# A fixed order for five engines: new words in the first layer, counted filler, and a new list for the expert layer

## The chip, the core and the metric

The kernel runs on one core of a Trainium2 chip. The core has a matrix engine (TensorE, PE in the profile), three engines for elementwise work (VectorE = DVE, ScalarE = ACT, GpSimd = POOL), a queue that only issues transfers here (SyncE = SP) and 16 DMA engines. The metric is the time of one execution on the device, in microseconds.

## What is computed

Three layers follow one another: pooled attention, a feed-forward layer with `h * cos(h)`, and a mixture of four experts, all in float32.

```python
# attention: 4 batches, 8 heads, 576 positions, head size 64, 32 memory slots
a = softmax(phi, axis=2)                       # over the positions
k_m = einsum('bhsm,bhsd->bhmd', a, k)
v_m = einsum('bhsm,bhsd->bhmd', a, v)
attn = softmax(matmul(q, k_m.T) / sqrt(64))    # over the 32 slots
x = matmul(attn, v_m)                          # then 2304 tokens x 512
# first feed-forward layer, 512 -> 2048 -> 512
h = x @ w_in
x = (h * cos(h)) @ w_out
# experts: 4 of 512 -> 1024 -> 512, weighted by domain_probs
p = domain_probs / domain_probs.sum(-1, keepdims=True)
for e in range(4):
    out += p[:, e:e+1] * (maximum(x @ w1[e], 0) @ w2[e])
```

## The kernel before

Nothing is scheduled by a compiler: the order of the instructions on every engine is written out in two tables of words. The work is cut into tasks, Python generators that yield one step (an `Op`) at a time. `Order.follow` reads the table word by word; each word names a task, and the task's next step is put on its engine. A step that two engines can do goes to the second one if the word has an apostrophe. Each engine runs its steps strictly in this order, and waits at a step until what the step needs is there. So a word's place sets what stands ahead of it on its engine, and nothing else.

`PLAN` (line 71) orders attention and the first feed-forward layer, with the first weights of the experts. Its tasks:

- `p`, `k`, `q`, `i`, `o` with digits are loads, one DMA each (a `k` is two, of 512 and 64 KB): phi, keys with values, queries, and slices of `w_in` and `w_out` as 64-bit words. p is 288 KB, q 576 KB, i and o 512 KB. All go through SP, which waits at a load until its buffer is free. There are 3 buffers for phi, 4 for k, 4 for q and 2 for raw weights (`RINGS`).
- `Abg` (`part`) is attention for batch b and group g of four heads: a maximum on DVE, the exponential on ACT, transposes on PE (`trans`, `pt`), pooling on PE (`pooled`, which needs both k of the group), a scaled copy on ACT (`kvs`), two transposes (`trans2`), a copy (`kvT`), scores on PE for either half of the positions (`score`, needs q), then a softmax over DVE, POOL and ACT (`sexp` is its exponential), a transpose, and a split in two parts for PE (`ahi` on ACT, `alo` on DVE or POOL).
- `wi`, `wo` (`narrow_in`, `narrow_out`) turn the 64-bit words into float32 weights on ACT and DVE.
- `P` (`project`) multiplies the pooled values by `w_in` (the values `vw`).
- `un.th` (`half`) is one unit of the first layer for half a batch: 12 matmuls (`hp`), then `h * cos(h)` in six steps, then four products `op` of six matmuls each with an addition (`ev`) each. `X` switches the on-chip memory over to the expert layer.

`LIST` (line 134) orders the expert layer: 64 units of a weight slice, two token groups each. `H` is the first product (with seven instead of eight block products), `R` the rectification, `P` and `Q` prepare the second product, `O` is the second product. For a pair of token tiles an `O` is PE's m1, m5, m6, m2, then a gather on DVE (e1: multiply by the expert's share and add to `acc`), then m7, m3, a second gather (e2), m4, and a third (e3). m7 overwrites what e1 reads, and m4 what e2 reads, so PE waits there for DVE. A single tile is one product `mm` and one gather. In the last two units, O62 (two pairs) and O63 (five tiles), each finished tile of the result is stored by a DMA of 256 KB on SP. `wa`, `wb`, `E`, `get`, `keep`, `fetch`, `park` and `unpark` build, store and load the weights' blocks and part of the accumulator.

PE also runs **filler**: matmuls of a 128x128 tile of ones whose result nobody reads, put ahead of steps at which PE waits. Each filler is two instructions in the trace. Fifteen run before the first word. In the kernel before, `Order.issue` reckons with its own cost figures how long PE will wait at a step that has a `fill`, and puts 0.75 of that time in filler ahead of it, plus counts from `more`; all of it before 75 us of its own reckoning.

Of the kernel before, what the change touches and what calls it, by code (L numbers as in the profile page):

```python
# [86 lines left out]
u2.0 u2.0 A30 A31 u2.1 A21 A31 u4.1 u2.1 u2.0 u3.1 u3.1 P4 u2.0 A31 A31 P4 u2.0 A30 A31 u2.1 u2.1 u4.1 u4.0 u2.1 A31
u3.1 u4.1 A30 u2.1 u2.1 u3.1 u2.0 A31 A30 u4.1 A30 u2.1 u2.0 wo2 u3.1 u3.1 u4.1 u3.1 A30 u3.1 u4.0 wi2 u3.1 u3.1
u4.1 u4.1' u4.0 X u4.0 G2 u6.1 wi2 wo2 u4.1 u6.1 u4.0 u6.1 u4.1' u4.0 u4.1 u6.1 wi2 u4.0' i21 u6.0 u4.0 G2 u6.1 G2'
G2' G2' u4.1' G2 u6.0 G2 u6.1 u6.0 u4.0' G2 u6.1' u4.0 wo2 G2 u6.0 G2 G2' u6.0 u4.0' G2 G2' u5.1 u6.0 u5.1 u6.1 G2  # L90
u6.1 wi2 u6.1 u6.0 u5.0 u6.0 u5.1 u5.1 u6.1' o21 wi2 u5.1 u5.0 wi2 u5.1 u5.0 G3 i30 u7.0 wo2 u5.1' u5.0 wo2 G2 u7.0
# [1801 lines left out]
```

## Time and profile before

| what | us |
|---|---|
| median of 3 runs | 1121.01 |
| lowest and highest | 1120.32, 1121.57 |
| the profiled execution | 1121.87 |
| its span, first to last instruction | 1120.1 |
| PE busy | 1104.5 |
| DVE, ACT, POOL busy | 865.1, 629.2, 577.7 |

The profiled execution is 0.86 us above the median; 1.8 us of it lie around the span. A matmul counts as busy from its start to its modelled end, and the next one starts before that end, so a busy PE is not PE at its peak: two starts must be compared. The trace holds every instruction in the order of the tables, so each one can be given to its word by counting.

### The profile page before, as it was taken

The page shows a single profiled execution, that of the slowest core. Times are in us where ns is not written, and L with a number is a line of the kernel's source. Part 1 is how long each engine was busy: PE and PEld are TensorE (multiplying, and loading weights), DVE is VectorE, ACT ScalarE, POOL GpSimd, SP SyncE. Part 2 cuts the span into 40 slices and gives each one's busy share as a digit, 9 for nine tenths or more (in the row PEclk, how much of TensorE's full clock was granted, in tenths as well). Part 3 has the DMA queues.
Part 4 walks back from the last instruction along what each step waited for, and adds up shares of the span by engine and source line. Part 5 has one row for each costly group of instructions (what it writes and reads, how often), then busy time and mean ns, then how long its engine had stood idle before and what let it go on. Part 6 is the DMA issues. An engine that isn't in the chain of part 4 may idle for free.

```text
span 1120.1 us, 22660 instructions
## 1 busy us (share of the span) xinstructions
PE 1104.5 (99%) x8981; PEld 1063.8 (95%) x8981; DVE 865.1 (77%) x1359; ACT 629.2 (56%) x1306; POOL 577.7 (52%) x569
## 2 busy tenths in 40 slices
...
GB/s 309 327 166 20 205 136 215 69 211 288 188 39 2 123 348 395 320 325 346 334 327 265 161 221 254 223 222 173 162 256 157 141 181 206 179 141 172 211 117 85
DMA packets 58554, 230.09 MB, mean 205 GB/s; under 512 B 6992, under 2 KB 17744, under 8 KB 44112
## 3 DMA queue, kind: packets, MB, share of 16 engines
...
## 4 chain that ended last, share of the span: by engine, by line
PE 90%; DVE 5%; DMA 2%; issue 1%; ACT 1%; POOL 0%; SPq 0%; DVEq 0%; ACTq 0%
PE op L506 48%; PE hp L506 33%; PE z L506 4%; DVE acc L1279 2%; PE vw_ps L793 1%; DVE ht L554 1%; PE spare L921 1%; DMA q<-in_qt_dram 1%; PE kvp L677 1%; DMA kv<-in_kv_dram 1%; PE sc L730 1%; DVE sm L554 1%; SPq L534 0%; DVE c L1265 0%; DVE acc L554 0%
## 5 line engine op out<-in xcount | busy, mean ns | idle before, releaser
L1279 DVE SCALAR_TENSOR_TENSOR acc<-op,p_all,acc 128x512 f32<-128x512 f32 x392 | 284.7, 746 | 120.9 <-PE op L506 118.7
L506 PE MATMUL hp<-x,wa 128*128 128x256 f32 (+1 forms) x2268 | 351.0, 295 | 0.1
L506 PEld LDWEIGHTS hp<-x,wa 128*128 128x128 f32 x2268 | 314.8, 188 | 2.0 <-DVE c L1265 0.3
L506 PE MATMUL op<-wt,ht 128*128 128x256 f32 x1464 | 228.8, 282 | 2.8 <-DVE acc L1279 2.6
L506 PE MATMUL op<-gt,wo 128*128 128x288 f32 x1536 | 218.1, 296 | 0.0
L506 PEld LDWEIGHTS op<-gt,wo 128*128 128x128 f32 x1536 | 208.1, 188 | 4.7 <-issue 2.4
L506 PEld LDWEIGHTS op<-wt,ht 128*128 128x128 f32 x1464 | 200.4, 188 | 5.6 <-DVE acc L1279 4.1
L506 PE MATMUL op<-wb,ht 128*128 128x256 f32 (+1 forms) x1182 | 203.2, 290 | 0.9 <-DVE acc L1279 0.8
L506 PEld LDWEIGHTS op<-wb,ht 128*128 128x128 f32 x1182 | 170.0, 188 | 5.9 <-DVE acc L1279 2.2
L554 POOL TENSOR_TENSOR sm<-c,sm 128x256 f32<-128x256 f32 x68 | 55.3, 814 | 145.8 <-DVE sm L554 118.8
L537 ACT ACTIVATE c<-c 128x256 f32<-128x256 f32 (+1 forms) x124 | 53.7, 443 | 126.7 <-DVE c L1265 126.6
L506 PE MATMUL hp<-attnT,vw 128*128 128x288 f32 x768 | 114.5, 298 | 0.3 <-DVE attnT L554 0.3
L554 POOL TENSOR_TENSOR ht<-sm,ht 128x512 fp32r<-128x512 f32 x72 | 97.8, 1366 | 31.8 <-ACT ht L537 28.2
L506 PEld LDWEIGHTS hp<-attnT,vw 128*128 128x128 f32 x768 | 106.4, 190 | 3.9 <-issue 2.0
L554 POOL TENSOR_TENSOR gt<-y,gt 128x576 fp32r<-128x576 f32 x41 | 60.0, 1463 | 79.2 <-ACT gt L537 76.2
L900 DVE TENSOR_TENSOR acc<-op,acc 128x576 f32<-128x576 f32 (+1 forms) x120 | 84.9, 711 | 17.3 <-PE op L506 16.1
L554 POOL TENSOR_TENSOR sm<-c 128x512 f32<-128x512 f32 x23 | 30.2, 1313 | 100.2 <-ACT c L537 83.5
L537 ACT ACTIVATE ht<-sm 128x512 fp32r<-128x512 f32 x122 | 75.2, 625 | 11.4 <-POOL sm L554 7.7
L554 POOL TENSOR_TENSOR ht<-c,ht 128x256 fp32r<-128x256 f32 (+1 forms) x61 | 67.1, 1105 | 25.1 <-ACT ht L537 25.1
L1265 DVE TENSOR_TENSOR c<-hp,u 128x320 f32<-128x320 f32 (+1 forms) x126 | 56.5, 453 | 22.0 <-PE hp L506 20.5
L537 ACT ACTIVATE ht<-c 128x256 fp32r<-128x256 f32 (+1 forms) x129 | 63.8, 516 | 13.6 <-PE op L506 12.2
L537 ACT ACTIVATE u<-hp 128x320 f32<-128x320 f32 (+1 forms) x126 | 50.5, 407 | 35.8 <-PE hp L506 35.5
...
## 6 DMA issues: line engine op xcount, KB each, us to landing
...
```

The lines of the kernel that those rows point to most:

```text
L506: nc.tensor.matmul(out=ps, lhsT=lt(a), rhs=rt(b), start=first and i == 0, stop=last and i == 2, skip_group_check=more,)
L537: return Op("ACT", ns, fn or (lambda: nc.scalar.activation(out=out, in_=in_, func=func, **kw)), *deps, table=table)
L554: eng.tensor_tensor(out=out, in0=in0, in1=in1, op=op)
L677: nc.tensor.matmul(out=kvp[32 * i:32 * i + 32], lhsT=es[:n, c, 32 * i:32 * i + 32], rhs=kv[i // 2][0][0][:, c, i % 2] if c < NC else kv[i ...
L730: nc.tensor.matmul(out=sc[32 * i:32 * i + 32, :TH], lhsT=kvT[b][p0:p0 + 64, 0, i, :], rhs=qt[p0:p0 + 64, i, :], start=True, stop=True,)
L793: nc.tensor.matmul(out=ps[32 * i:32 * i + 32, g, j * FS:j * FS + FS], lhsT=kvT[b][64 * g:64 * g + 64, 1, i, :], rhs=wi[s][0][64 * g:64 * g ...
L900: e = yield dve(155 + 301 * nd, lambda: nc.vector.tensor_tensor(out=dst, in0=op[:, :, :TH], in1=dst, op=ALU.add), o)
L921: nc.tensor.matmul(out=bank, lhsT=ones, rhs=ones, start=True, stop=True, skip_group_check=True)
L1265: return dve(157 + 1.045 * n, lambda: nc.vector.tensor_tensor(out=out, in0=ps, in1=sb, op=ALU.add), *deps)
L1279: nc.vector.scalar_tensor_tensor(out=dst, in0=ps, scalar=pe, in1=dst, op0=ALU.mult, op1=ALU.add)
```

## The change

Three things change, in the tables and in how filler is counted; no step is added or taken away, and each engine's total of steps stays but for those that move between two engines.

1. `PLAN` has the same 1462 words in another order (25 with the apostrophe set differently). Loads are among them: k000, k001 stand right behind p00; i00, i01 behind k011; q01, o00, i10 and p31 later, k110, k100 and k101 earlier. After the eighth unit the order on PE is that of before.
2. Filler is no longer reckoned. `FILLS` gives the count for each of PE's first 37 steps, 42 fillers in all (the trace of before holds 57).
3. `LIST` has the same 3646 words in another order, with 135 apostrophes set differently. Most words move by fewer than 10 places. At its end the products of O62 and O63 and the nine stores stand in another order.

```diff
--- before.py
+++ after.py
 PLAN = """
-p00 p11 k001 A00 k001 A00 A00 k000 A00' k000 A00 A00' A00 A00 A00 A00 p01 q00 A01 p10 i00 A11 A00' A10 A00 A00 q01
-A01 A01 A11 A00 A00' A00 A11 A01' A11 o00 A01 k010 A11 k010 A00 A01 k011 wi0 A10 k011 p20 A00 wi0 A00 A00 wi0 A00
-i01 A00 k111 A00 A00 p21 A01 A00 k110 k111 A01 A11' wo0 k110 wo0 A00 A11 A00 wo0 A00 A01 A00 A10 wi0 A01 A20 A00 o01
-A00 A00 wi0 A01 A01 A10 wi0 A01 A00 i10 P0 A01 A10 k100 A20 A01 P0 k100 A01 A21 P0 A01 A21 A01 k101 A11 A01' A01
-A10' A11 A01 A01 k101 p31 A10 A01 A20 A20 wo0 A11 q10 wi1 A20 A01 A20' A11 u0.0 A01 wo0 A01' wi1 A10 A01 A21 u0.0
-wo0 A01 u0.0 A01 wo0 wi1 u0.0 A11 q11 A01 A31 A01 A10 wo0 p30 A10 A11 A21 A01 u0.0 A10 k200 k200 A11 A11 k201 wo0
-A10 k201 wo0 A11 A01 i11 wo0 A10 u0.0 k210 A10 A30 A11 A21 A31 A10 A11 A30 P1 u0.0 wi1 A10 A10 A20 k211 A21 A11 u0.1
-A20 A11 A20 u0.0 wi1 A20 A10 u0.0' u0.1 u0.0 k210 u0.0' A20' A11 A21 A10 wi1 k211 u0.0 A21 q20 u0.0' P1 A10 A11 u0.1
-A11 A21 k301 P1 u0.0 u0.0' A31 A10 A11 A21 q21 A31' A20 A21 A30 k301 A10 o10 A20 u0.1 A31 A21 k300 P2 A10 A30 A20
-A21 A21 u0.1 A10' A20 A30 u0.1 P2 u0.1' u1.0 A21 u1.0 u0.1 wo1 u0.1' P2 u0.1 u1.1 u1.0 wo1 wo1 u1.0 u1.0 u0.1' u1.1
-A21 o11 u1.0 u1.1 u0.1 u0.1' u0.1 wo1 u1.1 u1.0 u3.0 A30' u1.0 A20 u0.1 u1.1 u1.0 u3.0 q31 k311 u1.1 A20 u1.1 u1.0
-u3.0 u1.0' q30 A31 i20 u1.0 u1.0 wo1 u3.0 A20 u3.0 u1.0 P3 wo1 A21 u1.0' k300 k310 A30 A20 P3 A20 wo1 A20 u1.1 A31
...
+p00 k000 k001 k000 k001 p01 q00 p10 A00 k010 A00 A00 A00 A00 p11 A00 A00 k010 A00 k011 A01 k011 i00 A00 A01 i01 A00
+A00 A10 q01 A00 A01 A00 A01 A01 k111 A00 A00 A11 p20 k111 A01 A11 A01 A00 A10 A01 A00 A00 A00 wi0 wi0 A01 wi0 A01 A00
+A11 o00 A01' wi0 wi0 k110 k110 A11 A11 A01 wi0 k100 A00 A01 A11' o01 A00 A00 A11 P0 A01 A00 A01 A10 A00 A01 A10' A10
+p21 A00 P0 k101 A01 A00 k101 A10' A00 A00 k100 P0 A00 A01 A00 A01 q10 A20 A11 A00 q11 wo0 A00' A20 A01 p31 A10 wo0 A01
+A11 A01 A01 A20 A01 wo0 A11 A20 wo0 A20 u0.0 A01 p30 A11' A20 A01 wo0 i10 A01 A21 k200 u0.0 A10 k200 wo0 k201 A01 wo0
+A01 k201 A11 A01' A21 wo0 A01 u0.0 A10 wo0 A01 A10 A20 i11 wo0 A11 A11 A10 A21 k211 wo0 A11 P1 u0.0 A11 A01 k211 A10
+A21 u0.0 A11 P1 A10 A10 u0.0 u0.1 k210 A10 A10 u0.0 A31 k210 A21 A11 q20 A30 A10 u0.0 wi1 A11 u0.1 q21 A11 A10 wi1 A11
+u0.0' u0.0 A20 A21 A10 A31 wi1 A30 A10 o10 A20 A10 u0.0' u0.0 A20 wi1 wi1 A11 A30 u0.1 A20' A11 wi1 u0.0' u0.0 A11 P1
+o11 k300 A21 A21 A30' P2 k300 u0.1 A10 k301 A21 A20 k301 u0.1 u0.0' A21 k311 A10 A31 A20 q30 A20 A21' A10' u0.1 A21
+A20 P2 A30 u0.1 u1.0 k310 A21 P2 k310 u0.1 u1.0 A20 wo1 u1.1 u1.0 A20 k311 u0.1 q31 u1.0 u0.1 A31 u1.0 u1.1 A21 wo1
+u1.0 u1.1 u3.0 A30' u0.1' u1.0 A21 u1.1 A30 A21 u0.1 u3.0 u1.1 u1.0 u3.0 u1.1 wo1 P3 u0.1' u1.1 u3.0 i20 A31 A30 A31
+u3.0 A21 u1.0 A20 u1.0 A31 A20 A21 u2.0 u1.0 A30 wo1 wo1 A21 P3 u0.1 wo1 A20 A30 o20 u1.0 u0.1' P3 A20 u3.0 u1.1 A30'
...
 LIST = """
...
-P62' O61.2 P62 P62 H63 O61.1 O61.0 O61.0 H63 H63 O61.0 P62' O61.1 O61.0 O61.1 O61.0 H63 H63 O61.0 P62' O61.1 O61.1
-O61.0 H63 O61.0 O61.1 H63 H63 R63 O61.1 O62.0 O61.1 H63 R63 R63 O62.0 R63 O62.1 O62.0 O62.1 R63 O62.0 O62.1 O62.0
-Q63.0 O62.1 Q63.1 Q63.0' O62.1 Q63.2 Q63.1' Q63.3 O63.0 O62.0 Q63.4 Q63.3 Q63.4' Q63.2 O62.0 O63.0 O62.0 O63.1 O62.0
-O62.1 O63.2 O63.1 O63.3 O63.2 O62.1 O62.1 O63.4 O62.1 O63.3 O62.1 O62.1 O62.0 O63.4 O62.0 O63.3 O62.1 O63.0 O62.0
-O62.1 O63.2 O62.0 O63.1 O63.4
...
+O61.2 O61.1 O61.0 O61.0 O61.1 O61.0 H63 O61.1 O61.0 H63 H63 R63 O61.0 O61.1 R63 R63 H63 O61.1 R63 O62.0 R63 O62.0
+O62.1 O62.0 O62.1 Q63.0 O62.0 O62.1 Q63.0 O62.0 Q63.1 O62.1 Q63.2 Q63.1' O62.1 Q63.3 O62.0 Q63.4 O63.0 Q63.3 Q63.2'
+Q63.4 O62.1 O63.1 O63.0 O62.0 O62.1 O62.1 O63.2 O62.1 O63.1 O62.1 O62.0 O63.0 O63.2 O63.3 O62.0 O63.2 O62.0 O63.4
+O63.3 O63.1 O63.3 O62.0 O63.4 O62.1 O62.1 O63.4 O62.0 O62.1 O62.0
 """.split()
...
@@ -324,8 +322,10 @@
 DMA_NS = 1.0 / 362.0
 DMA_LAG = 2700.0
 DMA_OPEN = 8
-FILL, FILL_NS, FILL_END = 0.75, 215.0, 75000.0
-LATE, LATE_NS = (14000.0, 35000.0), 1000.0
+FILLS = (
+    0, 0, 3, 3, 2, 0, 0, 10, 4, 0, 1, 0, 1, 0, 0, 0, 10, 0, 0, 0, 0, 0, 1, 0, 3, 0, 0, 0, 0, 0, 0, 0, 2, 0, 0,
+    0, 2,
+)
 
 
 class Order:
@@ -341,7 +341,7 @@
         self.left = {}
         self.quiet = set()
         self.log = []
-        self.more = [0, 0, 2, 0, 4]
+        self.fills = list(FILLS)
         self.stall, self.slack, self.late = 0.0, ({},) * 4, False
 
     def add(self, name, rank, gen):
@@ -410,13 +410,11 @@
             op.end = self.bus + DMA_LAG * 0.5
             self.landed.append(op.end)
         else:
-            if op.fill and t < FILL_END:
+            if op.fill:
                 bank, free = (self.spare, None) if self.spare is not None else op.fill
-                late = max((d.end + LATE_NS for d in op.deps if "SP" in getattr(d, "engs", ("SP",)) and LATE[0] < d.end < LATE[1]), default=0.0)
                 if task[3][0] == "P":
-                    self.spare, late = None, 0.0
-                more = self.more.pop(0) if self.more else 0
-                for _ in range(more + int(FILL * (max(t, late) - max(self.at[eng], free.end if free else 0.0)) / FILL_NS)):
+                    self.spare = None
+                for _ in range(self.fills.pop(0) if self.fills else 0):
                     self.filler(bank)
             self.at[eng] = t + ns
             if eng in op.port:
```

The order of PE's, DVE's and SP's last steps, read from the end of either table:

```
PE before   O62.1:m2 O63.0 O62.0:m7 O62.0:m3 O63.1 O63.2 O63.3 O62.1:m7 O62.1:m3 O63.4 O62.1:m4 O62.0:m4
PE after    O62.1:m2 O63.0 O63.1 O62.0:m7 O62.1:m7 O62.1:m3 O63.2 O62.0:m3 O63.3 O63.4 O62.0:m4 O62.1:m4
DVE before  O62.0:e1 O63.0 O62.0:e2 O62.1:e1 O63.1 O63.2 O62.1:e2 O63.3 O63.4 O62.1:e3 O62.0:e3
DVE after   O62.0:e1 O62.1:e1 O63.0 O62.1:e2 O63.1 O63.2 O62.0:e2 O63.3 O63.4 O62.1:e3 O62.0:e3
SP before   O62.1:e2 O62.0:e2 O63.3 O63.0 O62.1:e3 O63.2 O62.0:e3 O63.1 O63.4
SP after    O62.1:e2 O63.0 O63.2 O62.0:e2 O63.1 O63.3 O63.4 O62.1:e3 O62.0:e3
```

(SP's words are the stores; each is named by the gather that it waits for.)

## Rows read from the trace of the kernel before

**Rows 1.** Page, part 1: busy us, share of the span, instructions.
```profile
PE 1104.5 (99%) x8981; PEld 1063.8 (95%) x8981; DVE 865.1 (77%) x1359; ACT 629.2 (56%) x1306; POOL 577.7 (52%) x569
```

**Rows 2.** Stretches: us, busy of PE, PEld, DVE, ACT, POOL; clock, DMA share, GB/s.
```profile
0.00:10.00 10.00, 7.87 (x73) 7.71 (x76) 1.83 (x5) 2.61 (x5) 0.70 (x6) 1.00 0.80 268
10.00:20.00 10.00, 10.00 (x107) 8.29 (x97) 7.60 (x19) 5.78 (x14) 1.61 (x3) 1.00 0.97 340
20.00:30.00 10.00, 10.00 (x163) 7.92 (x162) 8.11 (x21) 5.61 (x13) 3.12 (x4) 1.00 0.99 337
30.00:40.00 10.00, 7.96 (x94) 5.36 (x96) 8.76 (x22) 9.22 (x15) 5.23 (x7) 0.96 1.04 361
40.00:50.00 10.00, 10.00 (x104) 7.12 (x97) 5.89 (x16) 5.42 (x13) 4.84 (x4) 0.70 0.95 309
50.00:60.00 10.00, 9.75 (x146) 7.20 (x145) 9.07 (x18) 8.14 (x14) 2.57 (x2) 1.00 0.93 329
60.00:130.00 70.00, 69.95 (x687) 64.87 (x692) 61.91 (x111) 52.67 (x86) 39.24 (x37) 1.00 0.34 109
```

**Rows 3.** Groups of PE instructions on ones (L921): busy us, mean ns, idle before.
```profile
L921 PE MATMUL spare<-ones 128*128 128x128 f32 x92 | 12.3, 278 | 0.0
...
L921 PE MATMUL kvp<-ones 128*128 128x128 f32 x16 | 2.1, 275 | 0.0
L921 PE MATMUL sc<-ones 128*128 128x128 f32 x6 | 1.2, 324 | 0.0
```

**Rows 4.** Timeline of PE, 5 to 60 us: start, us, instruction, count [idle before].
```profile
27.77 1.08 PE L677 MATMUL kvp<-kv,es 128*32 128x128 f32 x32
...
31.35 0.30 PE L658 MATMUL pt<-ident,phi 128*64 128x128 f32 x1 [1.04 <-ACT es L551]
31.41 1.82 PE L506 MATMUL hp<-attnT,vw 128*128 128x288 f32 x12
33.07 0.83 PE L921 MATMUL kvp<-ones 128*128 128x128 f32 x6
...
38.35 0.69 PE L730 MATMUL sc<-q,kvT 64*32 64x288 f32 x8 [0.64 <-DMA q<-in_qt_dram]
...
41.97 1.11 PE L793 MATMUL vw_ps<-wi,kvT 64*32 64x256 f32 x16
43.00 3.19 PE L506 MATMUL hp<-attnT,vw 128*128 128x288 f32 x12
46.13 1.08 PE L677 MATMUL kvp<-kv,es 128*32 128x128 f32 x32
...
50.28 1.08 PE L677 MATMUL kvp<-kv,es 128*32 128x128 f32 x32
...
51.65 1.06 PE L506 MATMUL op<-gt,wo 128*128 128x288 f32 x6
...
53.29 0.69 PE L730 MATMUL sc<-q,kvT 64*32 64x288 f32 x8
53.93 0.66 PE L651 MATMUL pe<-ident,phi 128*128 128x128 f32 x4
...
58.94 1.34 PE L506 MATMUL op<-gt,wo 128*128 128x288 f32 x9
```

**Rows 5.** Timeline of DVE, 43 to 51 us.
```profile
48.78 0.75 DVE L747 TENSOR_REDUCE ssm<-st 128x18 f32<-128x576 f32 x1 [3.52 <-ACT st L537]
```

**Rows 6.** PE's waits from 130 us on: us, times, longest.
```profile
PE op L506 <- DVE acc L1279: 3.5, 7, 0.9
```

**Rows 7.** Timeline of the end.
```profile
1110.75 3.47 DVE L1279 SCALAR_TENSOR_TENSOR acc<-op,p_all,acc 128x512 f32<-128x512 f32 x5 [1.36 <-PE op L506]
1111.53 5.16 SPq L534 DMA_DIRECT2D out_dram<-acc  x9
```

**Rows 8.** DMA issues near 1111.5 (first store) and 1116 us: count, KB, us to landing.
```profile
out_dram<-acc SPq DMA_DIRECT2D x1, 256.0 KB, 2.1
...
out_dram<-acc SPq DMA_DIRECT2D x2, 256.0 KB, 3.0
```

More of the change, by code (lines that the diff above doesn't have):

```diff
@@ L87 @@
[L87 to L91, printed above, removed]
@@ new lines @@
+u1.0 u1.1 u3.0 A30' u0.1' u1.0 A21 u1.1 A30 A21 u0.1 u3.0 u1.1 u1.0 u3.0 u1.1 wo1 P3 u0.1' u1.1 u3.0 i20 A31 A30 A31
+u3.0 A21 u1.0 A20 u1.0 A31 A20 A21 u2.0 u1.0 A30 wo1 wo1 A21 P3 u0.1 wo1 A20 A30 o20 u1.0 u0.1' P3 A20 u3.0 u1.1 A30'
+u2.0 A31 u1.0' u1.1 wo1 A20 u2.0 A30 A31 wo1 A30 A30 u2.1 A30 u3.0' u2.0 A30 u1.0 u2.1 A21 u2.0 A20 u1.1 A21 u2.1 A31
+u3.1 u1.1' wo1 u1.0 A31' u2.1 A20' wo1 u2.1 u3.1 wo1 A21 A31 u2.0 A31 A31 P4 A21 u2.0 A31 wo2 u1.1 A31 u3.0 u3.1 u1.1'
+A31 u3.1 u3.0 u3.0 A30 u3.0 u3.0 u1.1 A21 u3.0 A31 u3.1 u2.0 u1.1' A31 P4 u2.0 u2.0 A30 A31 u3.0 u2.0 u2.1 A31 P4 u2.0
@@ L133 @@
+u29.1 R1 u29.1 R1 u28.0 u28.1 u30.1 R1 u29.1 u30.1 u29.1 u30.1 u28.1 u28.1 R1 u30.1 u29.0 R1 u28.1 u29.1 B u29.0 B
+u30.1 u29.0 u31.1 u30.1' u29.0 B u29.1 u29.1 u31.1 u29.0 u31.1 B u29.0 u30.1 u29.1 u31.1 R1 u31.1 B u30.0 u29.0 u31.1
+u30.1 B' B u31.1 u30.1 u30.0 B' u31.0 R1 B' R1 u29.0 u30.0 B u30.1 u31.0 B u31.0 u29.0 u29.0 u31.0 u30.0 u31.0 u31.1
+u29.0 u31.0 B u31.0 u31.1 u31.1 u30.0 B u31.0 u30.0 u31.1 B u30.0 u31.0 u31.0 B' B u30.0 B u31.0 B u30.0 u30.0 u30.0
 """.split()
 LIST = """
[L135 removed]
@@ new lines @@
+wb11' R21 O20.1 wb11' wb11 O20.0 O20.0 P21' H22 P21 wb11' P21 O20.1 H22 O20.0 O20.1 wb11' P21 P21 H22 P21 O20.1 H22
+wa12' wb12 O20.0 P21 P21 O20.1 O20.0 H22 H22 H22 O20.0 O20.1 P21' P21 O20.1 O20.0 P21 H22 O20.1 H22 O20.0 wa12 O20.1
+H22 R22 O21.0 O20.1 O21.0 H22 R22 wa12' O21.1 keepwa11 wa12' wa12 wa12 R22 Q21.2 O21.0 R22 R22 O21.1 Q21.2' unpark
+wa12 O21.0 wa12' O21.0 O21.2 P22' P22 wa12' O21.1 wa12' H23 P22' O21.0 P22 P22 P22 H23 H23 P22' P22 P22 O21.1 O21.2
+O21.1 H23 H23 wa12' O21.0 O21.1 H23 H23 O21.0 O21.1 O21.0 O21.1 H23 O21.1 O21.0 O21.1 O21.0 H23 wb12 wa13 wb12 wb12
@@ new lines @@
+P22 P22 wb12 H23 H24 wb12' R23 R23 wb12 O22.0 O21.1 O22.0 H23 wb12' wb12 R23 wb12 O22.0 wb12' R23 O22.1 keepwb11 R23
+O22.1 O22.0 O22.1 O22.0 P23 H24 H24 P23 O22.0 O22.1 H24 H24 wa13 wb13 O22.1 H24 P23 O22.0 O22.0 P23 P23 P23 P23' H24
+O22.1 O22.1 O22.1 H24 P23 P23' O22.0 P23 O22.1 O22.0 P23 H24 H24 R24 Q23.2 O22.0 O22.1 R24 R24 H24 Q23.2 O22.1 R24
+O23.0 wa13 keepwa12 R24 O23.0 keepwt11 P24 P24 O23.1 wa13' O23.2 O23.0 P24' wa13 O23.0 P24' P24 P24 H25 O23.2 O23.0
+O23.1 P24' H25 H25 wa13 P24 P24' P24 O23.0 H25 H25 O23.1 wa13 H25 wa13 wa13' wa13 O23.0 P24 H25 O23.1 O23.0 O23.1
```

375 lines of the change are left out of this document (181 added, 194 removed).

## Prediction

> **What bounds the kernel now.** I read the page's busy shares first, then stretches of the span, then TensorE's timeline of the first 60 us, its waits, and the end. PE is busy for 1104.5 of 1120.1 us [rows 1], so time can come off only where PE runs filler, runs slowly, waits, or has stopped. There are three such places. *The start:* from 30 to 50 us PE lists 94 and 104 matmuls in 10 us, the granted clock is 0.96 and 0.70 of full, and the DMA engines are busy 0.97 to 1.04 of their time from 10 to 40 us [rows 2]. Matmuls on ones (filler) cost 12.3 + 2.1 + 1.2 = 15.6 us [rows 3]. So the start is bound by loads, and by half a clock after a thin stretch of PE. *The middle:* from 60 us on PE is busy all the time [rows 2], but waits seven times for a DVE gather, 3.5 us together [rows 6]. *The end:* the last gathers end at 1110.75 + 3.47 = 1114.22 us, yet nine stores are issued in one row from 1111.53 to 1116.69 [rows 7]; the last is issued one mean issue (5.16 / 9 = 0.57) before, near 1116.1, and lands 3.0 us later [rows 8], at 1119.1.
>
> The profiled execution took 1121.87 us (span 1120.1, 1.8 around it). The median is 1121.01, 0.86 lower. The sum below is made in the profiled execution and moved down by that 0.86.
>
> **Part 1: order of the first layer and counts of ones.** I go by landings. Sizes are from the code: p 288 KB, k 512 + 64, q 576, i and o 512. A load lands when the bytes up to its end have moved, by the GB/s of the stretches [rows 2], plus a lag. The lag has one good row: A11's second scores start at 38.35 us, after waiting for q11 [rows 4]. The list of before has 11,488 KB = 11.76 MB up to q11, moved at 36.4, so the lag is 1.9 us (an estimate, +-0.6). The stretches move 2.68, 3.40, 3.37, 3.61 and 3.09 MB, so 6.08 MB by 20 us, 9.45 by 30, 13.06 by 40.
>
> Landings in the new order: k110's tail (7,584 KB = 7.77 MB) 25.0 + 1.9 = 26.9. Last tail of k10 (9,536 KB) 32.8. q10 (10,112 KB) 34.4. q11 (10,688 KB, since i10 and p31 no longer stand ahead) 36.0. k201's tail (12,928 KB) 42.5. k210's tail (14,592 KB) 48.0. q21 (15,744 KB) 51.8. From k200 to i11 the bytes ahead are those of before, so these land no earlier: PE only stops being behind its loads.
>
> PE in the new order. Durations are from start to start [rows 4]: pooled 1.37 (50.28 to 51.65), hp 1.66 (31.41 to 33.07), so an op of six matmuls 0.83, scores 0.64 (53.29 to 53.93), four transposes 0.5 and two 0.25 (estimated from their row), a vw 1.0 (41.97 to 43.00); two ones 0.27 (12.3 / 46 [rows 3]). A11's pooled matmuls wait for k110 and run 26.9 to 28.3 (before from 27.77). Scores, transposes and u0.0's hp follow, near 30.0 to 31.6 (before from 31.41). A10 pooled waits for k10: 32.8 to 34.2; A11's scores wait for q10, 34.4, and q11, 36.0 to 36.6 (before from 38.35). A21's transposes 0.5, P1 1.0, two scores 1.3: u0.1's hp runs 39.4 to 41.1. Before, it ran from 43.00 for 3.19 us at half clock. A pt, ones and two ops (2.2) end at 43.3, A20 pooled at 44.7 (before 46.13 + 1.37 = 47.5). Op, ones, transposes and op (2.9) end at 47.6; now **PE waits for k210**: A21 pooled 48.0 to 49.4 (before to 51.65). P2 1.0, scores 0.64, transposes 0.75, then scores behind q21, 51.8 to 52.4, scores 0.64, a pt: u1.0's hp runs 53.2 to 54.9. Before, the first op after it starts at 58.94 [rows 4]. The new order has by then left A21's second scores and A31's pt (0.74) for later, so it stands where before stood at 58.94 when it is 55.6: **the lead is 3.3 us**. Bounds, from 0.6 of lag either way and an attention chain up to 1 us late: 1.8 to 5.0.
>
> What else that needs. DVE must bring A10's attention (its last step `alo`) by 53.2. Before, DVE stood 3.52 us until 48.78 for ACT's exponential of A10 [rows 5], which was queued on ACT behind a step that needs A20 pooled (46.13 [rows 4]). In the new ACT order it stands ahead of that step, so this stall goes. What is late next is A10's `ahi`, on ACT behind A21's `kvs`, which needs A21 pooled (49.4): kvs, an eviction and ahi (estimates of 0.5 to 0.7 each), then `alo` (0.7, as DVE's other steps of this shape [rows 5]), end near 52.1, 1.1 before it is needed.
>
> Moves on other queues. *SP:* p11 now stands ahead of k010's tail and waits for a phi buffer that A00's pt frees, within the first 10 us; 3,104 KB are queued ahead, moved only at 11.5, so the DMA engines don't run dry. o00 stands ahead of k110 and waits for i00's narrowing, near 19.5; 6,496 KB ahead are moved at 21.7. *ACT:* A01's `kvs` now stands behind the narrowing of i00 (4,544 KB, landing 17.7), and A01's transposes, its first scores and u0.0's hp behind that. PE waits for k110 until 26.9 anyway, which hides it; without that cover, the nearest row is PE's wait of 1.04 us for ACT at 31.35 [rows 4]. I take 0 and keep +1.0, which is in the bounds. *POOL* gets the same kinds of steps in another order: 0.
>
> The ones: 57 before (114 instructions in [rows 3], two each), 42 in the new list, so 15 x 0.27 = 4.0 us fewer. They stand where PE waits for a load, so alone they are worth nothing; ten remain ahead of A01's and of A11's pooled matmuls. What they do bear on is the clock. It lost 0.04 x 10 / 0.5 = 0.8 us from 30 to 40 and 6.0 us from 40 to 50 [rows 2], so it ran at 1.2 instead of 2.4 GHz from about 39.2 to 46.0, after PE had waited for ACT at 31.35 and for q11 at 38.35 with little between [rows 4]. The Trainium skill ("TensorE: Matmul & The Clock Gate", section "HAM oscillation — how this bites in real kernels") says that short bursts of matmuls between DMA waits throttle the array again and again; it speaks against fewer ones, and by it the sum would be rival A's.
>
> **Part 2: list of the expert layer.** *The end.* PE's last products are the same (O63.4, then an m4 of each pair of O62), so the last gather ends at 1114.22 + 0.1, as O62.1's now waits for the very last m4. What changes is who is queued behind whom on SP. Before, SP's first word is the store after O62.1's second gather, the seventh of the last eleven gathers, and eight stores stand behind it. In the new list O62.1's m7 and m3 come before O63.2, this gather is the fourth of eleven, and the stores nearly follow the gathers, the two last ones last. Gathers come every 3.47 / 5 = 0.69 us and an issue takes 0.57 [rows 7], so no store waits for another: the last is issued at 1114.35. Landing takes between 2.1 (the first, queues empty) and 3.0 us (the last two of nine) [rows 8]; I take 2.4, nearer the first, as few stores are under way: 1116.75 instead of 1119.1. **Gain 2.35**, bounds 1.7 and 2.7.
>
> *The rest of the list.* Most words move a few places, and 135 change between POOL and DVE. The seven waits [rows 6] come from gathers queued behind DVE steps; for three of them (O8.1, O23.1, O29.0) the new list puts 0.4 to 0.7 us more PE work between product and reader. Ends: all seven go (-3.5), or as many come (+3.5). I take 0, as kinds and numbers of steps are the same. The weights' transfers keep their order but for neighbours; `unpark`'s second half and two stores of unit 29 move far down, where they were due long before.
>
> **Sum.** 1121.87 - 3.3 - 2.35 + 0 = 1116.2 in a profiled execution; less 0.86: **1115.3**.
>
> **Rivals.** *A, the clock still falls* between 31 and 46 us. For: fewer ones, and PE still waits near 31.6, 34.2 and 35.5. Against: hp, scores and vw stand closer together than before. Price: u0.1's hp 3.19 instead of 1.66, 1.5 us, or P1, scores and pooled about as much; the waits for k210 take part of it: 1.2 to 1.8. Time 1116.8. *B, the lead is given back before 130 us:* DVE is busy 9.07 of 10 us from 50 on and 61.9 of 70 after that [rows 2], so it may become the bound, and only the end is left: 1121.0 - 2.35 = 1118.7. Against: DVE's 3.52 us stall goes. *C, slower:* the reordered list makes PE wait for gathers (m7, m4) more often. A wait is 0.5 us on average [rows 6]; to cancel 5.7 us and be 2.3 slower takes 16 more of them among the 122 pairs of products: 1123.3. Against: a doubling (seven more, 1118.8) is the most that the unchanged kinds of steps suggest. *D, more than forecast:* loads land 0.6 earlier, and half of the seven waits go: 1112.7.
>
> **How the numbers follow.** Forecast 0.57, with its own range 1113.6 to 1117.0; A 0.13; B or C's doubling 0.14; C 0.05; D 0.11. The range takes in A, D's near side and half of B: 1112.5 to 1118.4. Within 0.2% of 1121.0 (1118.8 to 1123.2, about what a measurement can tell from no change) lie half of B and the short side of C, 0.11; slower 0.04; faster 0.85.
>
> **What would show it.** Right: A21 pooled starts within 0.8 us of 48.0; u0.1's hp takes 1.7 us at full clock; u1.0's hp ends near 54.9; the nine stores go out one by one, and the last lands about 2.5 us after the last gather's end. Wrong: a PEclk below 0.9 before 50 us (A), PE waiting for DVE between 55 and 130 us (B), more than 7 us of waits for `acc` (C), a landing 3 us or more after the last issue.

## The result, and the profile after

The changed kernel takes 1109.0 us (1108.8 to 1109.6, four executions) against 1121.3 of the kernel before beside it: a ratio of 0.9889, 95% interval 0.9874 to 0.9905. That is 12.3 us faster; the forecast was 5.7, and its range ended at 1112.5. The profiled execution took 1109.16 us, its span 1107.4.

The page's first part (busy us, share, instructions), against [rows 1]:

```profile
PE 1097.0 (99%) x8951; PEld 1059.7 (96%) x8951; DVE 865.9 (78%) x1361; ACT 628.0 (57%) x1307; POOL 578.8 (52%) x566
```

Stretches of the start, columns as in [rows 2]:

```profile
10.00:20.00 10.00, 9.49 (x114) 7.60 (x110) 6.39 (x16) 5.70 (x13) 1.38 (x2) 1.00 1.01 373
20.00:30.00 10.00, 8.26 (x116) 5.64 (x109) 9.17 (x25) 6.22 (x16) 4.24 (x6) 1.00 1.04 341
30.00:40.00 10.00, 9.75 (x132) 7.10 (x130) 9.46 (x23) 9.05 (x16) 7.19 (x9) 1.00 1.03 365
40.00:50.00 10.00, 9.45 (x162) 7.69 (x161) 9.50 (x22) 9.72 (x21) 4.84 (x4) 1.00 1.03 373
```

The clock (third from the end) stays at 1.00, where it was 0.96 and 0.70 from 30 to 50. The loads run at 373 GB/s from 10 to 20 and from 40 to 50 us, where they ran at 340 and 309.

PE's timeline, for [rows 4]:

```profile
25.85 1.08 PE L675 MATMUL kvp<-kv,es 128*32 128x128 f32 x32
...
31.64 1.08 PE L675 MATMUL kvp<-kv,es 128*32 128x128 f32 x32
...
35.02 0.69 PE L728 MATMUL sc<-q,kvT 64*32 64x288 f32 x8
...
37.78 1.86 PE L504 MATMUL hp<-attnT,vw 128*128 128x288 f32 x12
...
46.57 1.08 PE L675 MATMUL kvp<-kv,es 128*32 128x128 f32 x32 [0.55 <-DMA kv<-in_kv_dram]
...
50.85 1.83 PE L504 MATMUL hp<-attnT,vw 128*128 128x288 f32 x12
```

These are A11 and A10 pooled, A11's second scores, u0.1's hp, A21 pooled and u1.0's hp. Each comes earlier than forecast (26.9, 32.8, 36.0, 39.4, 48.0, 53.2), the last by 2.35 us. By u8.1's first products the kernel is 5.9 us ahead of before (133.65 before, 127.73 now):

```profile
133.65 1.09 PE L506 MATMUL hp<-attnT,vw 128*128 128x288 f32 x7
127.73 0.96 PE L504 MATMUL hp<-attnT,vw 128*128 128x288 f32 x6
```

PE's waits for gathers from 130 us on, for [rows 6] (us, times, longest):

```profile
PE op L504 <- DVE acc L1277: 0.9, 2, 0.5
```

The lead grows from 5.9 us at the first product of the expert layer's unit 10 to 9.8 at that of unit 28. Then the end, for [rows 7] and [rows 8]:

```profile
1102.12 2.12 DVE L1277 SCALAR_TENSOR_TENSOR acc<-op,p_all,acc 128x512 f32<-128x512 f32 x3 [0.65 <-PE op L504]
```

```profile
1098.36 6.25 SPq L532 DMA_DIRECT2D out_dram<-acc  x9
```

```profile
out_dram<-acc SPq DMA_DIRECT2D x9, 256.0 KB, 2.1
```

The last gather ends at 1104.24 and the span 3.2 us later, instead of 5.9. So the three gains in the two traces are 5.9 at the start, 3.9 in the middle and 2.7 at the end.

### The profile page after: what moved, and what is told of

The parts are those of the page before. It is cut to its first block, busy times and chain, and to the rows that moved or that the text cites. A ratio compares the mean times of both kernels' runs of the same rounds, so it can differ in the third digit from the quotient of the medians.

```text
span 1107.4 us, 22591 instructions
## 1 busy us (share of the span) xinstructions
PE 1097.0 (99%) x8951; PEld 1059.7 (96%) x8951; DVE 865.9 (78%) x1361; ACT 628.0 (57%) x1307; POOL 578.8 (52%) x566
## 4 chain that ended last, share of the span: by engine, by line
PE 92%; DVE 3%; DMA 3%; ACT 1%; issue 0%; POOL 0%; SPq 0%; DVEq 0%
PE op L504 50%; PE hp L504 35%; PE z L504 4%; DMA kv<-in_kv_dram 2%; PE vw_ps L791 1%; DMA raw<-in_w_in_dram 1%; PE kvp L675 0%; DVE acc L1277 0%; DVE acc L552 0%; DVE x L552 0%; PE sc L728 0%; DVE sm L552 0%; DVE ht L552 0%; ACT ht L535 0%; DVE acc L1275 0%
## 5 line engine op out<-in xcount | busy, mean ns | idle before, releaser
L552 POOL TENSOR_TENSOR gt<-y,gt 128x576 fp32r<-128x576 f32 x44 | 65.2, 1482 | 84.4 <-ACT gt L535 81.6
L552 POOL TENSOR_TENSOR sm<-c 128x512 f32<-128x512 f32 x31 | 40.8, 1317 | 125.5 <-ACT c L535 95.9
L552 POOL TENSOR_TENSOR ht<-sm,ht 128x512 fp32r<-128x512 f32 x65 | 88.7, 1367 | 17.6 <-ACT ht L535 17.5
L535 ACT ACTIVATE op<-op 128x256 f32<-128x256 f32 x122 | 44.5, 368 | 48.1 <-PE op L504 47.9
L535 ACT ACTIVATE ht<-c 128x256 fp32r<-128x256 f32 (+1 forms) x129 | 63.9, 515 | 13.3 <-PE op L504 12.3
```

Source lines behind the costliest of these rows:

```text
L535: return Op("ACT", ns, fn or (lambda: nc.scalar.activation(out=out, in_=in_, func=func, **kw)), *deps, table=table)
L552: eng.tensor_tensor(out=out, in0=in0, in1=in1, op=op)
```

## The experiments

**The three parts, one at a time.** `new_plan` has the changed `PLAN` with its ones and the old `LIST`; `new_list` the reverse; `end_only` the old kernel with the last 65 words of the new `LIST`; `stores_moved` only SP's words there:

```diff
 SP's stores, each named by its gather
-O62.1:e2 O62.0:e2 O63.3 O63.0 O62.1:e3 O63.2 O62.0:e3 O63.1 O63.4    (first one behind the 7th gather)
+O63.0 O62.0:e2 O63.1 O63.2 O62.1:e2 O63.3 O63.4 O62.1:e3 O62.0:e3    (each right behind its gather)
```

> The changed PLAN with its counted ones, and LIST as before. Theory (three gains that add up, read from the two traces: 5.9 us at the start, 3.9 in the middle, 2.7 at the end): u8.1's first products start near 127.7 instead of 133.65 and nothing else changes, so 1121.0 - 5.9 = 1115.1. Rival (the forecast's sizes: the start is worth 3.3 and what is seen beyond it needs the new LIST too): 1117.7. Rival (DVE or a later stage gives the lead back): above 1119.

> PLAN and the 57 ones as before, the changed LIST. Theory (three gains that add up): middle 3.9 and end 2.7, so 1121.0 - 6.6 = 1114.4, with at most two waits of PE for a gather after 130 us. Rival (the forecast: the middle is worth nothing by itself, the end 2.35): 1118.7. Rival (the middle's gain comes from the earlier start, as DVE and POOL then run ahead of PE): 1118.3 and about seven such waits.

> As before, but the last 65 words of LIST (the products of O62 and O63, their gathers and the nine stores) stand in the changed order. Theory: the tail from the last gather's end to the span's end falls from 5.9 to 3.2 us, so 1121.0 - 2.7 = 1118.3. Rival (the forecast's landing time of 2.4): 1118.7, not to be told from it by the time, but by the tail. Rival (part of the end's gain comes from the words ahead of these 65): less than 1.5 us, above 1119.5.

> As before, but each of the nine stores of O62 and O63 stands on SP right behind its gather; the order on PE, DVE, ACT and POOL is that of before. Theory (the end is SP's queue alone: the first store stood behind the seventh of eleven gathers and eight more behind it): all of the end's gain without any move of a product, 1121.0 - 2.5 = 1118.5. Rival (the order of products and gathers is needed, because five stores in the last five gathers still bunch up): a gain below 1.3, above 1119.7.

Measured (ratio to before on the same chip, 95% interval): `new_plan` 1116.7 us, 0.9957 (0.9943 to 0.9971); `new_list` 1113.8, 0.9938 (0.9922 to 0.9954); `end_only` 1117.5, 0.9967 (0.9954 to 0.9980); `stores_moved` 1117.3, 0.9962 (0.9947 to 0.9976). The parts add up: 0.43 and 0.62% are nearly the 1.11% of the whole. The median of before beside a run lies between 1120.1 and 1121.9, since its clock falls in a changing share of its executions (next part); at full clock it is 1119.8 to 1120.2 in every group of runs, so runs of different groups are compared below by their times and not by these ratios. The end is SP's queue alone. In `stores_moved` DVE's last five gathers and SP's nine stores read

```profile
1108.77 3.46 DVE L1275 SCALAR_TENSOR_TENSOR acc<-op,p_all,acc 128x512 f32<-128x512 f32 x5 [1.36 <-PE op L502]
```

```profile
1103.93 8.65 SPq L530 DMA_DIRECT2D out_dram<-acc  x9
```

```profile
core 0: 1115.4 us, clock 0.999
```

The gathers are as in [rows 7], 3.46 instead of 3.47 us long; only the stores begin 8.3 us ahead of their end instead of 2.7. From the last gather's end (1112.23) to the span's end it takes 3.2 us, as in the changed kernel and in `end_only` (1112.57 to 1115.7). The new order of products adds nothing.

**The half clock of before is a matter of chance.** `end_only` has PE's first 60 us as before, yet

```profile
30.00:40.00 10.00, 7.64 (x90) 5.22 (x88) 8.07 (x21) 8.84 (x15) 5.24 (x7) 1.00 1.04 359
40.00:50.00 10.00, 10.00 (x150) 7.63 (x150) 9.05 (x22) 7.91 (x17) 6.41 (x6) 1.00 1.03 352
```

the clock holds, and the loads move 352 instead of 309 GB/s from 40 to 50. The kernel before ran 91 times beside the experiments: 48 executions had a mean clock of 0.998 or 0.999 (median 1120.0 us), 43 had 0.993 to 0.997 (median 1123.0); a group of runs on one chip had from 5 of 18 to 12 of 19 of the latter. Against 1120.0 the changed kernel gains 11.0 us, not 12.3. The changed `PLAN` with its 42 ones, in all kernels that have it, fell below 0.998 in 1 of 48. u8.1's first products start at 131.45 in `end_only` and at 133.65 in before, so in these two traces the fall costs 2.2 us. Against `end_only`, the changed `PLAN` (128.06 in `new_plan`) gains 3.4, and against 1120.0 at full clock 1116.7 is 3.3 less. All kept traces agree: this place is reached at 131.02 and 131.45 with the first layer of before at full clock (`stores_moved`, `end_only`), at 133.65, 134.09 and 134.47 with the fall (before, `phi_ring_four`, `new_list`), and at 126.58 to 128.63 in the eight with the changed `PLAN` and its ones (mean 127.97). By the means the order gives 3.3 us and the fall costs 2.8; the 5.9 of the two traces holds both. Two kernels ask what the ones do: `no_ones` is `new_plan` without any of the 42, `more_ones` is before with 17 more where PE waits between 30 and 39 us.

```diff
-FILLS = (0, 0, 3, 3, 2, 0, 0, 10, 4, 0, 1, 0, 1, 0, 0, 0, 10, ...)
+FILLS = (0, 0, 0, ...)
```

> The changed PLAN with none of its 42 ones (the fifteen ahead of the first word stay), LIST as before; 1116.6 with them. Theory C (the ones are there for the clock): without them the granted clock falls in a stretch before 50 us, and the time rises by the price of such a fall, 2 to 5 us, 1118.5 to 1121.5. Rival N (the order of steps alone keeps PE dense enough): the clock stays at 1.00 and the time within 0.5 of 1116.6. Rival P (some ones stand in PE's way): 1116.0 or less.

> As before, with 17 more ones, 74 in all: one ahead of A01's second scores, four ahead of A20's pt, two each ahead of A21's transposes, A11's first scores and A10's transposes, five ahead of A11's second scores, one ahead of A10's second scores; PE waits there between 30 and 39 us. Before, the mean clock of 37 executions was 0.997 or lower in 16 (1121.2 to 1125.4 us) and 0.998 or 0.999 in 21 (near 1120.0). Theory (the half clock near 39 us comes from PE's thin stretch, and is a matter of chance at these densities): every execution at 0.998 or higher, 1119.5 to 1120.8. Rival (it does not depend on ones there): four in ten executions at 0.997 or lower, as before. Rival (ones in the way): all near 1121.5 with a full clock.

`no_ones`: 1118.1 us, 0.9976 (0.9967 to 0.9986), and its clock falls for most of 20 us:

```profile
10.00:20.00 10.00, 5.55 (x58) 3.21 (x59) 6.61 (x16) 4.86 (x11) 1.34 (x2) 0.66 1.03 369
20.00:30.00 10.00, 6.72 (x92) 3.46 (x91) 7.73 (x23) 5.65 (x15) 3.48 (x5) 0.67 1.03 348
30.00:40.00 10.00, 8.55 (x111) 6.01 (x112) 8.84 (x21) 7.89 (x16) 5.25 (x8) 0.81 1.04 353
```

Theory C holds, at a lower price than expected: 1.4 us by the medians (2.0 at u8.1 in the traces) for (0.34 + 0.33 + 0.19) x 10 / 0.5 = 17 us at half clock, and PE waits 5.1 us there for keys and values anyway. `more_ones`: all 11 executions at 0.998 or 0.999, so ones at these places do keep the clock; but 1123.0 us, 1.0023 (1.0013 to 1.0032), against 1119.5 to 1120.8 expected. u8.1 starts at 134.05, 2.6 and 3.0 us later than in the two traces at full clock without them: the 17 ones cost as much as the fall.

**Are the loads' order or the steps' order the gain of part 1?** Each was put with the other's old order.

```diff
 steps_old_loads_new: PE, DVE, ACT, POOL as before; SP:
-p00 p11 k001 k001 k000 k000 p01 q00 p10 i00 q01 o00 k010 ...
+p00 k000 k001 k000 k001 p01 q00 p10 k010 p11 k010 k011 ...
 steps_new_loads_old: the other way round
```

> PE, DVE, ACT and POOL in the order of before, with its 57 ones and its LIST; the first layer's loads go out on SP in the changed order (but i10 one place earlier, ahead of p30, and i21 and o20 in another order). Executions at full clock are to be compared: about 1120.1 for before, 1116.5 with all of part 1. Theory L (the gain comes from loads that are ahead sooner: k110, k100, q10 and q11 land 1.5 to 2 us earlier, because o00, i10 and p31 are no longer ahead of them): 1117.6 to 1118.3, A11's pooled matmuls near 26. Theory S (it comes from the order of PE's steps, which were behind their loads): 1119.5 or more.

> The changed order of steps on PE, DVE, ACT and POOL with its 42 ones, LIST as before; the loads go out in the order of before (but i01 ahead of p20 and k111, and o20 after k310's tail). Theory L: A11's pooled matmuls stay near 27.5 and its second scores near 38, and most of part 1's gain is gone, 1118.5 to 1119.5. Theory S: u8.1's first products within 1 us of those with all of part 1 (128.1), 1116.5 to 1117.5. If each alone gives less than half, they need one another: 1119 or more for both kernels.

1129.5 us, 1.0087 (1.0072 to 1.0101), and 1134.6, 1.0123 (1.0106 to 1.0140): neither is worth anything alone, and both lose. What came is the third sign, 1119 or more for both: they need one another. None of the 11 executions kept the clock (0.987 to 0.995), so a part of both losses may be the fall's, but 9 and 14 us are more than the 2.8 that it costs above. Stretches of `steps_new_loads_old`, and SP's longest wait:

```profile
20.00:30.00 10.00, 9.20 (x98) 6.79 (x99) 3.96 (x11) 4.03 (x10) 2.10 (x3) 0.76 0.67 224
30.00:40.00 10.00, 6.65 (x86) 5.13 (x84) 9.62 (x26) 6.74 (x15) 3.71 (x5) 1.00 0.41 135
```

```profile
SPq L530 <- PE kvp L673: 10.3, 3, 9.9
```

The DMA engines are busy 0.67 and 0.41 of the time. A load waits on SP for a buffer, 9.9 us at one pooled product: a step that now comes later frees it, and all loads behind it wait too. In the other kernel SP's longest waits are 8.8 and 7.5 us, for two narrowings.

**Why the loads land earlier than reckoned.** For 12,352 KB, k200's tail lands at 41.81 in `end_only` and at 40.14 in `new_plan`; over the traces it is 41.25 to 41.87 in five with the loads of before and 38.49 to 41.00 in eight with the changed `PLAN` and its ones. Before, SP stands from 11.9 to 16.3 at p20 (a phi buffer) and until 18.8 at i01 (i00's raw buffer, freed by its narrowing); eight transfers are under way when it stops. SP's waits of the first 60 us in before show the two stands as the longest of their rows (us, times, longest):

```profile
SPq L534 <- PE pt L658: 7.9, 3, 4.4
SPq L534 <- DVE wi L596: 3.7, 2, 2.1
```

`phi_ring_four` was meant to give phi a fourth buffer, but the tile itself kept three, so it is the kernel before once more (1119.9 us, 0.9986, 0.9972 to 1.0000). `phi_four` has the fourth, `i01_own_buffer` also a buffer of its own for i01.

```diff
-RINGS = dict(phi=3, ...
+RINGS = dict(rawx=1, phi=4, ...
-        ring = R[dict(p="phi", k="kv", q="q", i="raw", o="raw")[kind]]
+        ring = R["rawx" if name == "i01" else dict(p="phi", k="kv", q="q", i="raw", o="raw")[kind]]
```

> As before, but with four buffers for phi instead of three. In executions at full clock (1120.0 for before) SP waits four times, 8.1 us, for a transpose of phi to free a buffer in the first 60 us. Theory (SP's waits for buffers thin the queue, and that is why the loads land 1 to 1.7 us later for equal bytes than in the changed order): that wait falls below 4 us, the transfers move 360 to 373 GB/s from 10 to 20 us instead of 350, k110's tail lands 0.8 us or more earlier than 28.4, and the time is 1118.8 to 1119.5. Rival (SP then stands at the next buffer, for i00's narrowing or for a k): the waits change their name, the landings stay, 1120.0.

> As before, but with four buffers for phi, in the ring and on chip. (In phi_ring_four only the ring had four, the tile kept three, so nothing had changed.) In executions at full clock, 1120.0 before. Theory (SP's waits for a phi buffer thin the queue of loads, and that is why loads land 1 to 1.7 us later for equal bytes than in the changed order): SP's waits for pt fall from 8.1 to below 4 us, 360 GB/s or more from 10 to 20 us (349 to 355 before), k110's tail lands by 27.6 instead of 28.4, 1118.8 to 1119.5. Rival (SP then stands at the next buffer): the waits change their name, landings within 0.3 us, 1120.0.

> As before, with four buffers for phi and a buffer of its own for i01, so that SP does not stand at p20 until 16.2 nor at i01 until 18.7 us (i01 waits there for i00's narrowing, as its buffer is i00's). In phi_four the transfers moved 232, 147, 191 and 299 GB/s in the four us from 18 to 22, against some 380 around them: about 650 KB or 1.7 us missing, as much as the loads land later than in the changed order. Theory (SP's stand at i01 empties the queue, and that is the dip): 340 GB/s or more in each of these four us, k110's tail by 27.2 instead of 28.2 to 28.4, k200's tail by 40.6 instead of 41.1 to 41.8. Rival (the dip is made by the loads themselves, whichever is first): it stays, landings within 0.3. For the time at full clock, 1120.0: 1119.0 to 1119.6 if the order of steps of before can use earlier loads, 1120 if not.

Stretches of one us, `phi_four`:

```profile
18.00:19.00 1.00, 1.00 (x12) 1.00 (x11) 1.00 (x4) 0.89 (x3) 0.37 (x1) 1.00 0.82 232
19.00:20.00 1.00, 1.00 (x12) 1.00 (x11) 0.96 (x6) 0.29 (x1) 0.73 (x2) 1.00 0.86 147
20.00:21.00 1.00, 1.00 (x14) 0.88 (x14) 0.97 (x4) 0.44 (x1) 0.49 (x1) 1.00 0.65 191
21.00:22.00 1.00, 1.00 (x37) 0.80 (x36) 0.93 (x5) 0.00 (x0) 0.00 (x0) 1.00 0.97 299
```

`i01_own_buffer`:

```profile
18.00:19.00 1.00, 1.00 (x12) 1.00 (x11) 0.96 (x5) 0.98 (x3) 0.68 (x1) 1.00 1.06 348
19.00:20.00 1.00, 1.00 (x11) 1.00 (x10) 0.97 (x5) 0.00 (x0) 0.73 (x2) 1.00 1.05 375
20.00:21.00 1.00, 1.00 (x19) 0.88 (x21) 1.00 (x2) 0.44 (x1) 0.18 (x1) 1.00 1.02 399
21.00:22.00 1.00, 1.00 (x36) 0.62 (x28) 0.93 (x4) 0.00 (x0) 0.26 (x1) 1.00 1.06 412
```

With phi alone the wait only changes its name: p20 goes out at 12.2, SP stands at i01 until 18.7, k200's tail lands at 41.13, and the time is 1120.5 (0.9997, 0.9987 to 1.0008). With both, the dip is gone, k200's tail lands at 40.40, nearly as early as in the changed order, and the kernel takes 1117.5 us (0.9973, 0.9963 to 0.9982), 2.5 less than 1120.0 and 2.3 less than the full-clock executions beside it, with the old order of everything. Its nine executions all kept the clock. In the one trace u8.1 starts at 129.92, 1.1 and 1.5 us earlier than in the two at full clock with the old buffers. So SP's stand was the dip, and a good part of the start (1.1 to 2.5 us of 3.3) was to be had by it alone.

**The middle.** The new `LIST` saves its time between units 10 and 28. Their first products are 207.0 us apart in `new_plan` and 202.6 in the changed kernel, which differs from it in `LIST` alone (busy of PE, PEld, DVE, ACT, POOL):

```profile
479.40:686.30 206.90, 203.88 (x1559) 199.64 (x1558) 174.55 (x268) 122.05 (x285) 131.89 (x125) 1.00 0.76 273
```

```profile
479.30:681.90 202.60, 202.58 (x1560) 199.59 (x1558) 169.79 (x271) 121.87 (x286) 130.33 (x122) 1.00 0.76 274
```

PE's idle time falls from 3.0 us to 0.02 and its busy time by 1.3, as matmuls around a wait are drawn out too. DVE is busy 4.8 us less with three more instructions. `new_list` has 202.4 with the old `PLAN`, so the earlier start isn't the cause. The place at O12.1 shows what is. In `new_plan` (DVE, POOL, PE):

```profile
530.85 1.51 DVE L550 TENSOR_TENSOR acc<-raw,acc 128x512 fp32r<-128x512 f32 x1
532.28 0.74 DVE L1275 SCALAR_TENSOR_TENSOR acc<-op,p_all,acc 128x512 f32<-128x512 f32 x1
```

```profile
530.52 1.29 POOL L550 TENSOR_TENSOR acc<-raw,acc 128x512 fp32r<-128x512 f32 x1 [0.54 <-ACT acc L533]
```

```profile
531.81 0.87 PE L502 MATMUL hp<-x,wa 128*128 128x256 f32 x6
533.08 0.97 PE L502 MATMUL op<-wt,ht 128*128 128x256 f32 x6 [0.40 <-DVE acc L1275]
```

Eb14's cl (a step that subtracts the high part of a block of weights to leave the low one; the l of a second product is of the same kind) starts on DVE while POOL works on the other one, and takes 1.51 us, ending 0.55 after POOL's; the gather behind it is late, and m7 starts 1.27 us after the matmuls ahead of it. In the changed kernel both cl are on POOL, and these matmuls read

```profile
531.30 0.87 PE L504 MATMUL hp<-x,wa 128*128 128x256 f32 x6
532.01 0.87 PE L504 MATMUL op<-wt,ht 128*128 128x256 f32 x6
```

0.71 apart: the 0.40 us of idle cost 0.56. Five kernels test this. `five_gathers` moves only the DVE steps ahead of the five late gathers that the new `LIST` cures:

```diff
 order on DVE (new PLAN, old LIST)
-P9.l3 O8.0.e2 c22 O8.1.e1 | Eb14.cl O12.1.e1 | Q15.2.l c12 O14.0.e2 | wb11.lt wa12.mix O20.1.e1 | wa13.l O23.1.e1
+O8.0.e2 c22 O8.1.e1 P9.l2 | O12.1.e1 Eb14.cl | c12 O14.0.e2 Q15.2.l | O20.1.e1 wb11.lt wa12.mix | O23.1.e1 wa13.l
```

(P9's l3 and l2 change engines by it.) Two kernels mix the two lists: the old places with the new engines of each step, and the reverse. Counted by step, 269 stand on the other engine; the prediction's 135 are those that go from POOL to DVE (in `PLAN` it is 41, not 25). And `five_segments` takes five stretches of the new `LIST`, 694 words around those gathers, into the old one; `all_but_five` is its complement.

> The changed PLAN, and LIST as before but for five places: P9's l3, Eb14's cl, Q15.2's l, wa12's mix with wb11's lt (and wb12's load), and wa13's l stand behind the gather that they stood ahead of on DVE (O8.1 e1, O12.1 e1, O14.0 e2, O20.1 e1, O23.1 e1); 1116.6 without this. Theory (the middle's gain is these five gathers, each late behind a DVE step that takes 1.2 to 1.8 instead of 0.7 us while POOL works): 1112.3 to 1113.0, waits for a gather after 130 us 4.0 down to 1.0 to 1.5 us. Rival (DVE has as much to do as before, so others come late instead): 1115 or more. Rival (the whole new order of LIST is needed, with its 135 steps that change engine): above 1114.5.

> The changed PLAN; LIST's words in the order of before, but each step that POOL or DVE can do is on the engine of the changed LIST (269 steps differ, 135 go from POOL to DVE and 134 the other way). 1116.5 with the engines of before; the changed LIST's middle is worth 4.3. Theory E (which engine a step is on decides how long DVE takes ahead of a gather): 1112.5 to 1113.5. Theory O (the places decide): 1115.5 to 1117.5. Theory B (places and engines fit only each other): 1118 or more, with more than seven waits for a gather after 130 us.

> As the changed kernel (1109.0), but each step of LIST that POOL or DVE can do is on the engine that it had before. Theory O (the places decide): 1109 to 1110. Theory E (the engines decide): 1112.5 to 1113.5. Theory B (they fit only each other): 1114 or more, with more than seven waits for a gather after 130 us.

> The changed PLAN; LIST as before, but five stretches of its words (559 to 597, 812 to 906, 940 to 1005, 1252 to 1416, 1466 to 1794, counted from 0; the same steps stand in each in both kernels) are those of the changed LIST, with its places and its engines. They hold the five gathers for which PE waited in the old LIST and not in the new. 1116.5 without them. Theory (places and engines must change together, but only around the late gathers): 4 us, 1112.0 to 1113.0, with two waits for a gather left. Rival (the gain needs LIST from its start on, as the steps of a weight are spread over several units): 1114.5 or more.

> The changed kernel (1109.0) with the words of before in the same five stretches of LIST. Theory (the middle's gain lies in these stretches alone): 4 us slower, 1112.8 to 1113.8, with seven waits for a gather. Rival (the rest of LIST carries it): 1111 or less.

`five_gathers`: 1115.2 us, 0.9958 (0.9942 to 0.9973), 1.5 less than `new_plan` (1.4 between units 10 and 28 in the traces) and not 4. The waits only moved on:

```profile
PE op L502 <- DVE acc L1275: 3.5, 6, 1.3
```

At O12 the gather now comes in time, but the cl behind it still meets POOL and takes 1.76 us, and the next gather (e2) is late instead. `old_order_new_engines`: 1126.9, 1.0053 (1.0038 to 1.0067). `new_order_old_engines`: 1125.4, 1.0032 (1.0019 to 1.0045), with

```profile
PE op L501 <- DVE acc L1274: 7.7, 13, 1.2
```

Theory B: places and engines fit only each other. Its sign, more than seven such waits, came in the second; the first has seven of 5.2 us together, and 3.3 us of waits for other steps that `new_plan` hasn't. `five_segments`: 1111.3, 0.9914 (0.9901 to 0.9928), two waits left:

```profile
PE op L502 <- DVE acc L1275: 1.0, 2, 0.6
```

`all_but_five`: 1114.7, 0.9944 (0.9931 to 0.9957), five waits, where 1112.8 to 1113.8 and seven were expected. Between units 10 and 28 the stretches give 4.6 us where they are put in (202.3 us for 207.0) and take 3.8 where they are taken out (206.4 for 202.6). So the middle's gain lies in those five stretches, in places and engines together; 1.1 us of what `all_but_five` loses come after unit 34 and are not explained.

**Can the changed kernel be made faster?** `after_two_gathers` moves the steps ahead of the two gathers that are still late; `after_o00_own` gives o00, SP's longest stand in the new order, its own buffer.

```diff
-P30.l4 X10.xl0 O29.0.e1 | R31.l3 O30.1.e1 O30.0.e2
+O29.0.e1 P30.l4 X10.xl0 | O30.1.e1 R31.l3 O30.0.e2
```

> As the changed kernel (1109.0, where PE still waits twice for a gather after 130 us, 0.9 together, at O29.0's m7 and O30.0's m4), but P30's l4 and X10's xl0 stand behind O29.0 e1, and R31's l3 behind O30.1 e1 instead of ahead of it. In the changed kernel the l4 takes 1.78 instead of 0.68 and the l3 1.90 instead of 0.48 us, as POOL's mix of X10 runs then. Theory (a lengthened DVE step ahead of the gather is what PE waits for): both waits go, 1107.6 to 1108.0. Rival (as with the five places: the lengthened step only makes the next gather late): 1108.6 or more.

> As the changed kernel (1109.0), with a buffer of its own for o00, for which SP stands from 14 to 19 us there. Theory (the changed order has its loads early enough at this stand, so little is missing: 360 GB/s from 19 to 20): landings 0.1 to 0.4 us earlier up to k110's tail, 1108.5 to 1109.1. Rival (what is left of SP's waits still sets the start): 0.7 us or more earlier, below 1108.4.

1109.5 us, 0.9897 (0.9882 to 0.9912), and 1110.6, 0.9908 (0.9894 to 0.9922): neither is told apart from the changed kernel's 0.9889, and the theories' 1107.6 to 1108.0 and 1108.5 to 1109.1 were missed. In the first, units 28 to 34 take 71.84 instead of 72.25 us and one wait of 0.4 is left, at the next gather; in the second k200's tail lands 1.1 us earlier (39.16 for 40.31), and u8.1 starts 0.5 earlier, both within the scatter of the traces with the same loads (38.49 to 41.00, 126.58 to 128.63). No version here beats it surely.

## Why the prediction was wrong

The direction and the three places were right, and rivals A, B and C did not come; two of the three terms were too small.

- **The rest of `LIST`, taken as 0, gave 3.9 to 4.4 us.** This is the step that failed most. The reason, that "kinds and numbers of steps are the same", says nothing on how long a DVE step takes, and that depends on whether POOL runs beside it. The number of steps that change engine was also read at half its size. The bound of 3.5 was too small too: it was the waits' idle time, while five of the seven waits went, and a wait costs more from start to start than its idle (0.56 for 0.40 at O12.1). The new places at O29.0, named as a reason for a gain, did not help: it is one of the two waits left.
- **The start, taken as 3.3, gave 5.9 against the profiled execution.** Here the landings failed: "go by the GB/s of the stretches" took for the chip's rate what was partly SP's doing. The rows that spoke of it were there: in [rows 2] the share falls to 0.95 where the clock is down, and SP's stands could have been read from the queue's waits. q10 was reckoned at 34.4 and its scores ran at 33.31, q11 at 36.0 and 35.02, k210 at 48.0 and 46.57; u1.0's hp came 2.35 us earlier than reckoned, which is nearly all of 5.9 - 3.3. A21 pooled at 46.57 is outside the 0.8 us around 48.0 that the prediction named as its sign. That from k200 to i11 loads "land no earlier" was wrong by 0.7 to 0.9 us.
- **The half clock** was reckoned as a fixed cost of the order. It is in 43 of 91 executions. By medians the start is worth 3.3 at full clock, and the rest of its gain is that the fall has become rare. That 3.3 is also the forecast number is chance: it was reckoned against an execution with the fall.
- **Rivals.** A (the clock still falls): not with the 42 ones; without any of them it does, to 0.66 to 0.81 in `no_ones`. The rule of the Trainium skill behind this rival ("TensorE: Matmul & The Clock Gate", section "HAM oscillation — how this bites in real kernels"), that short bursts of matmuls between DMA waits throttle the array again and again, agrees with that trace. B (the lead given back by 130 us): no, 5.9 at u8.1 and at unit 10. C: no, but it is real: the two mixed lists show that an unlucky pairing costs 10 to 16 us. D named both causes, 0.6 us earlier landings and half of the waits gone; they were about twice as large. By its own terms its sum is 1113.0, not 1112.7.
- **The end, 2.35, gave 2.7**, its upper bound. The reason held to the letter: the queue's order alone. The landing was 2.1 (median of nine), not 2.4, as the stores no longer run together.
- **The ones:** 42 instead of 57, and the clock held better. That fewer ones alone are worth nothing is not shown: no run has 42 of them in the order of before. What `no_ones` shows is that these 42 are worth 1.4 us, by the clock.

In sum 2.6 + 3.9 + 0.35 = 6.9 us of the 7.0 by which the profiled execution is below the forecast's 1116.2.
